# Scores of a head pair in three full PSUM tiles, and three score regions per two pairs

## The chip, the cores and the metric

The kernel runs on one core of one Trainium2 chip. The metric is the device time of one execution in microseconds (us); a kernel's time is the median of several runs.

## What is computed

Blockwise causal attention over 8 batches of 8 heads (576 positions, head size 64, mask blocks of 64), then a layer of two products whose larger value goes through a third. Inputs and output are fp32.

```python
scores = q @ k.T / sqrt(64)                  # per batch and head
scores = where(pos_i // 64 >= pos_j // 64, scores, -1e9)
attn = exp(scores - max); attn = attn / (sum(attn) + 1e-9)
a = attn @ v                                 # [8, 8, 576, 64]
x = a.transpose(0, 2, 1, 3).reshape(4608, 512)
out = maximum(x @ w1, x @ w2) @ w_out        # w1, w2: 512x1024; w_out: 1024x512
```

## The kernel before

All matmuls are in bf16. The order of the work on every engine is written out by hand: each engine's queue runs in the order in which the source calls come.

**Attention.** Two heads that share 128 partitions (64 each) are a pair `p`; there are 32 pairs, four in a batch, and two neighbouring pairs are a group `g` (16 groups). For each pair:

- q and k come in on SP's queue as fp32 (`load_qk`, L109; for later groups a one-column memset on POOL holds the load back, L116), and POOL casts them to bf16 (`cast`, L127). TensorE transposes them (`transposes`, L302: 18 matmuls for q or for k of a whole group), DVE and ACT copy the result to `qT` and `kT` (L309). The table `T_AT` (L459) gives each pair `s` of the main loop one such step: q of the next group for even `s`, k of the next group for odd `s`.
- `scores` (L315) computes keys by queries: the stationary operand is a chunk of 128 keys (64 rows of head dimension by 128 columns), and the moving operand is the run of queries that may see it. The two heads of the pair are two matmuls on the two halves of the partitions. 576 keys are five chunks, the last of 64 keys; its missing 64 columns are zeros, for which `kT` is 64 columns longer (L95). The query runs are 576, 448, 320, 192 and 64 columns long, 1600 in all.
- ACT takes the exponential of a PSUM tile of scores into `aT` (`exp`, L325), and POOL sets to zero the half of a diagonal block that the mask forbids (`mask`, L330).
- A pair's 1600 columns go through PSUM in four tiles from the pool `ps_s`, which holds two tiles of two banks each. `burst_a` (L360) fills two of them with 512 columns per head, `burst_b` (L371) a third with 512 and a fourth with the 64 of the last chunk; each then has its exps and masks.
- `av` (L382) multiplies `aT` with v, which has a column of ones that gives the sum (24 + 6 matmuls of 65 columns, 128x128 weights, L398), and DVE divides (L404, L405). `x_out` (L410) transposes two pairs' results into `xT` (L420, L422). This runs `LAG = 2` pairs behind the scores.

**The layer.** `h_unit` (L181) makes 128 columns of `max(x w1, x w2)` for a span of tokens: four matmuls of up to 512 columns for each of the two (L196), DVE takes them out (L203, L205). `y_unit` (L209) makes 128 tokens of the output: eight matmuls of 512 columns (L214), taken out by ACT (DVE for the first two spans, L220) and stored on SP's queue. `fill(n)` (L280) issues the next `n` steps of this list, in units of one 512-column matmul, as far as tokens are ready. The pool `ps_m` (four tiles of one bank) serves transposes, `av`, `x_out`, h and y alike.

**The main loop** (L547) runs over pairs `s` from 4 to 31: `x_out` if one is due, `burst_a`, a fill of about half of `n`, the transposes of `T_AT`, `burst_b`, the copies of the transposes, `pool_work(s)` (L442: loads and casts for later groups, v loads), `av` of pair `s - 2` in two parts with a short fill between, and the rest of the fill. `fill_of` (L435) sets `n` so that the ready work is spread until the next batch's tokens are ready. Pairs 0 to 3 stand ahead of the loop in an order of their own (L467 to L544).

Of the kernel before, what the change touches and what calls it, by code (L numbers as in the profile page):

```python
# [8 lines left out]
FP32 = mybir.dt.float32  # L9
BF16 = mybir.dt.bfloat16  # L10
AF = mybir.ActivationFunctionType
# [3 lines left out]
def kernel(  # L15
# [10 lines left out]
    nc = tc.nc  # L26

    B, H, S, D = q.shape
    P = 128
    BLK = 64  # L30
    HP = H // 2
    NPAIR = B * HP
# [5 lines left out]
    scale = 1.0 / float(D) ** 0.5  # L38
# [6 lines left out]
    NG = NPAIR // 2  # L45
    GPB = HP // 2

    CB = [0, 448, 768, 960, 1024]  # L50
    AW = 1600
    APAD = 64
    NCH = 5
# [5 lines left out]
    def a_col(p, c, t):  # L59
        if p >= HP:  # L60
            return CB[c] + t * P
        late = t * P >= QCUT
        return t * P + {
            0: 384 - QCUT if late else 0, 1: 704 - QCUT if late else 256 - P,
            2: 1024 - QCUT, 3: 1408 - 3 * P, 4: 1344 - 4 * P,
        }[c]
# [9 lines left out]
    tiles = [(carry[i] + w) // P for i, (_, w) in enumerate(spans)]  # L76

    wpool = ctx.enter_context(tc.tile_pool(name="wpool", bufs=1))
    ring = ctx.enter_context(tc.tile_pool(name="ring", bufs=1))
# [7 lines left out]
    ps_s = ctx.enter_context(tc.tile_pool(name="ps_s", bufs=2, space=bass.MemoryType.PSUM))  # L87
# [4 lines left out]

    NV, NA, NT = 3, 4, 4
    qT_r = [ring.tile([P, S], BF16, name=f"qT{r}") for r in range(NT)]
    kT_r = [ring.tile([P, S + APAD], BF16, name=f"kT{r}") for r in range(NT)]  # L95
    vv_r = [ring.tile([P, NCH, H, D + 1], BF16, name=f"vv{r}") for r in range(NV)]
    aT_r = [ring.tile([P, 2, AW + APAD], BF16, name=f"aT{r}") for r in range(NA)]
    xT = ring.tile([P, NDM, NTOK + BLK], BF16, name="xT")
# [24 lines left out]
    def cast(nm, g, parts):  # L123
        t = raws.pop((nm, g)).rearrange("p s (t d) -> p t s d", d=D)
        qk_n[nm, g] = n = qkn.tile([P, RPP, 2, D], BF16, name=f"{nm}n")
        for copy, j0, j1 in parts:
            copy(out=n[:, j0:j1], in_=t[:, j0:j1])  # L127

    def load_v(b, c):
        rows = min(P, S - c * P)  # L130
        nc.gpsimd.dma_start(  # L131
            out=vv_r[b % NV][:rows, c, :, :D],
            in_=v[b, :, c * P:c * P + rows, :].rearrange("h p d -> p h d"),
        )

# [23 lines left out]
    make_identity(nc, ident)  # L159
    for r in range(NV):  # L160
        nc.vector.memset(vv_r[r][:, :, :, D:D + 1], 1.0)
        nc.vector.memset(vv_r[r][BLK:, NCH - 1, :, :], 0.0)
    for r in range(NT):
        nc.vector.memset(kT_r[r][:, S:], 0.0)
    for r in range(NA):
        nc.vector.memset(aT_r[r][BLK:, :, CB[4] + 512:], 0.0)
        nc.vector.memset(aT_r[r][:BLK, :, AW:], 0.0)
    cast("q", 0, ((dve, 0, 7), (pool, 7, RPP)))
    cast("k", 0, ((act, 0, 5), (dve, 5, RPP)))
    for c in range(2):  # L170
        load_v(0, c)
# [101 lines left out]
    def ready():  # L273
        n, total = at[0], 0.0
        while n < len(steps) and steps[n][1] <= done_tokens[0]:
            total += steps[n][2]
            n += 1
        return int(total)

    def fill(n):  # L280
        while n > 0 and at[0] < len(steps) and steps[at[0]][1] <= done_tokens[0]:
            u, _, cost = steps[at[0]]
            next(u)
            n -= cost
            at[0] += 1
# [28 lines left out]

    def scores(p, ps, col, c, q0, w, m=P):  # L315
        qT, kT = qT_r[p % NT], kT_r[p % NT]
        for hh in range(2):
            r = slice(hh * D, (hh + 1) * D)
            nc.tensor.matmul(  # L319
                ps[:m, hh, col:col + w], kT[r, c * P:c * P + m], qT[r, q0:q0 + w],  # L320
                start=True, stop=True,
            )

    def exp(p, ps, w, a0, m=P):
        nc.scalar.activation(  # L325
            out=aT_r[p % NA][:m, :, a0:a0 + w], in_=ps[:m, :, :w], func=AF.Exp, scale=scale,
        )

    def mask(p, a0, eng=None):
        (eng or nc.gpsimd).memset(aT_r[p % NA][BLK:, :, a0:a0 + BLK], 0.0)  # L330

    def burst(p, parts, a0):
        u = ps_s.tile([P, 2, 512], FP32, name="ps_s", tag="s")
        w = 0
        for c, q0, n in parts:
            scores(p, u, w, c, q0, n)
            w += n
        exp(p, u, w, a0)
# [18 lines left out]
        for a in (1024, 1408):  # L357
            mask(p, a, eng)

    def burst_a(p):  # L360
        u0 = ps_s.tile([P, 2, 512], FP32, name="ps_s", tag="s")
        scores(p, u0, 0, 0, 0, 512)
        u1 = ps_s.tile([P, 2, 512], FP32, name="ps_s", tag="s")
        scores(p, u1, 0, 0, 512, 64)
        scores(p, u1, 64, 1, 128, 448)
        exp(p, u0, 512, 0)
        mask(p, 0)
        exp(p, u1, 512, 512)
        mask(p, 576)

    def burst_b(p):  # L371
        u2 = ps_s.tile([P, 2, 512], FP32, name="ps_s", tag="s")
        scores(p, u2, 0, 2, 256, 320)
        scores(p, u2, 320, 3, 384, 192)
        u3 = ps_s.tile([P, 2, 512], FP32, name="ps_s", tag="s")
        scores(p, u3, 0, 4, 512, 64)
        exp(p, u2, 512, 1024)
        mask(p, 1024)
        mask(p, 1344)
        exp(p, u3, 64, 1536, m=BLK)  # L380

    def av(p, ts):  # L382
        b, hp = divmod(p, HP)
        vv = vv_r[b % NV]
        a = aT_r[p % NA]
        n = len(ts)
        h0 = hp // 2 * 4 + hp % 2
        if p % 2 == 0 and ts[0] == 0:
            xps[p // 2] = xpool.tile([P, NCH, 2, 2, D], BF16, name="xp")
        xp = xps[p // 2]  # L390
        po = ps_m.tile([P, n, 2, D + 1], FP32, name="ps_o", tag="m")
        n_mm = 2 * sum(t + 1 for t in ts)
        mm = 0
        for gi, t in enumerate(ts):
            for hh in range(2):
                for c in range(t + 1):
                    a0 = a_col(p, c, t)
                    nc.tensor.matmul(  # L398
                        po[:, gi, hh, :], a[:, hh, a0:a0 + P], vv[:, c, h0 + 2 * hh, :],
                        start=(mm == 0), stop=(mm == n_mm - 1),  # L400
                    )
                    mm += 1
        rec = small.tile([P, 3, 2, 1], FP32, name="rec")
        nc.vector.reciprocal(rec[:, :n, :, 0], po[:, :, :, D])  # L404
        nc.vector.tensor_mul(  # L405
            xp[:, ts[0]:ts[0] + n, :, p % 2], po[:, :, :, :D],
            rec[:, :n].to_broadcast([P, n, 2, D]),
        )
# [23 lines left out]
    LAG = 2  # L432
    KEEP = 6

    def fill_of(s):  # L435
        if s >= NPAIR - LAG:
            return 27
        left = 10 - s if s < 10 else 4 - (s - 2) % 4
        return -(-max(0, ready() - KEEP) // left)


    def pool_work(s):  # L442
        g, i = divmod(s, 2)
        if s == 4:
            pass
        elif s == 5:
            load_qk(5, (SP, SP), gated=True)
            cast("q", 4, ((pool, 0, RPP),))
        else:
            if i == 1 and g + 3 < NG:  # L450
                load_qk(g + 3, (SP, SP), gated=True)
            if g + 1 + i < NG:
                cast("kq"[i], g + 1 + i, ((pool, 0, RPP),))
            nb, j = divmod(s + 2, HP)
            if nb < B:
                for c in ((0, 1), (2, 3), (4,), ())[j]:
                    load_v(nb, c)
# [4 lines left out]
    def t_pair(s):  # L462
        outs = [transposes(nm, g, (dve, act)) for nm, g in T_AT.get(s, [])]
        return lambda: [f() for f in outs]
# [15 lines left out]
    for c in range(2, NCH):  # L480
        load_v(0, c)
# [62 lines left out]
    fill(3)  # L544

    x_due = []
    for s in range(HP, NPAIR):  # L547
        g, i = divmod(s, 2)
        if x_due:
            x_out(x_due.pop())  # L550
        n = fill_of(s)
        burst_a(s)
        if s == HP:
            av(3, [2, 3, 4])
            fill(5)
            x_out(1, 2, NCH)
            n = fill_of(s)
        n_a = n // 2 if n > 12 else n * 3 // 5
        n_b = n // 6
        fill(n_a)  # L560
        copy_out = t_pair(s)
        burst_b(s)
        copy_out()
        pool_work(s)
        if s >= HP + LAG:
            p = s - LAG
            av(p, [0, 1])
            fill(n_b)
            av(p, [2, 3, 4])
            if p % 2:  # L570
                x_due.append(p // 2)
        else:
            fill(n_b)
        fill(n - n_a - n_b)
    for p in range(NPAIR - LAG, NPAIR):
        if x_due:
            x_out(x_due.pop())
        av(p, [0, 1])
        fill(5)
        av(p, [2, 3, 4])  # L580
        fill(11)
    x_out(NG - 1)
    fill(len(steps))
# [36 lines left out]
```

The softmax here doesn't subtract the row's maximum and nothing guards it: scores larger than these inputs give would overflow.

## Time and profile before

| what | value |
|---|---|
| runs | 288.96, 289.13, 289.14 us; median 289.13 us |
| the profiled execution | 288.79 us, of which the span from the first to the last instruction is 286.7 us |
| granted TensorE clock | 1.000 |
| TensorE busy | 280.0 us, 98% of the span, 3197 matmuls |
| DVE, ACT, POOL busy | 186.7, 137.0, 101.5 us |
| L196 (h), L214 (y) | 140.7 and 69.6 us on TensorE |
| L398 (attention by v), L319 (scores) | 40.5 and 34.7 us on TensorE |
| L325 (exp) on ACT | 128 instructions, 100.3 us |

Times in the profile are us from the start of the span unless marked ns. PE is TensorE's matmul row, PEld its weight loads. A group's line gives the source line, the engine, the operation, what it writes and reads, the size of the stationary operand in rows*columns, the moving operand, and the count. Matmuls are pipelined: the end of one in the records lies after the start of the next, so the distance of two starts is what a matmul takes from the engine. In a timeline the columns are start, length and the group of like instructions that follow each other; brackets hold the idle time of that engine ahead of it and what ended it.

### The profile page before, as it was taken

What the parts mean: (1) busy time and instruction counts of PE and PEld (TensorE: products, weight loads), DVE (VectorE), ACT (ScalarE), POOL (GpSimd) and SP (SyncE); (2) the same over time, 40 slices, a digit from 0 to 9 for tenths busy, and PEclk for the clock granted to TensorE, in tenths of its full rate; (3) what the DMA queues carried; (4) which work ended last, traced back from release to release, by engine and by line L of the source; (5) the groups of instructions that cost most, each with busy time, mean ns of one, the idle gap of its engine ahead of it and who ended that gap; (6) DMA issues with size and microseconds to landing.
All of it is one profiled execution on the core that took longest, in us unless ns stands there. A gap on an engine that the chain in (4) does not pass through costs nothing.

```text
span 286.7 us, 7670 instructions
## 1 busy us (share of the span) xinstructions
PE 280.0 (98%) x3197; PEld 146.1 (51%) x3197; DVE 186.7 (65%) x390; ACT 137.0 (48%) x194; POOL 101.5 (35%) x243
## 2 busy tenths in 40 slices
PE   7799999999999999999999999999999999999995
PEld 3457666555554545545445445454554554444443
DVE  6867878578785666766665666566665766455430
ACT  3786575775665455555545555545545100010112
POOL 2995547547535432344225532543111000000000
PEclk9999999999999999999999999999999999999999
DMA  7999999977954692479266684555101011011114
GB/s 266 259 210 233 169 259 257 247 231 86 192 133 82 141 144 88 156 77 237 49 201 75 171 115 105 130 59 67 43 37 39 37 39 74 37 63 49 53 60 146
DMA packets 55939, 36.67 MB, mean 128 GB/s; under 512 B 38752, under 2 KB 43232, under 8 KB 55904
## 3 DMA queue, kind: packets, MB, share of 16 engines
q0 software_dynamic: 41728, 7.87, 34.0%
q1 hardware_dynamic: 13760, 27.66, 28.4%
q10 hardware_dynamic: 416, 0.66, 0.7%
q8 instruction: 25, 0.41, 0.6%
q14 instruction: 10, 0.08, 0.1%
HBM read 34.60 MB, written 9.44 MB: 154 GB/s over the span
## 4 chain that ended last, share of the span: by engine, by line
PE 93%; DMA 4%; DVE 1%; POOL 0%; issue 0%; ACT 0%
PE ps_h L196 44%; PE ps_y L214 21%; PE ps_o L398 12%; PE ps_s L319 8%; DMA vv<-in_v_dram 2%; PE ps_qT L302 2%; DMA qraw<-in_q_dram 2%; PE ps_xe L420 2%; PE ps_kT L302 2%; PE ps_w L291 1%; PE ps_y L230 1%; PE ps_xo L422 0%; DVE g L205 0%; DVE xp L405 0%; POOL vv L131 0%; DVE qT L309 0%
## 5 line engine op out<-in xcount | busy, mean ns | idle before, releaser
L196 PE MATMUL ps_h<-xT,w_sb 128*128 128x512 bf16 (+3 forms) x640 | 140.7, 358 | 0.1
L325 ACT ACTIVATE aT<-ps_s 128x1024 bf16<-128x1024 f32 (+3 forms) x128 | 100.3, 832 | 59.5 <-PE ps_s L319 56.9
L196 PEld LDWEIGHTS <-w_sb 128*128 128x128 bf16 x640 | 57.7, 98 | 55.6 <-issue 5.5
L203 DVE CAST h<-ps_h 128x512 bf16<-128x512 f32 (+3 forms) x80 | 50.9, 636 | 44.6 <-PE ps_h L196 42.9
L214 PE MATMUL ps_y<-wo_sb,g 128*128 128x512 bf16 x280 | 69.6, 379 | 0.0
L330 POOL MEMSET aT<- 64x128 bf16 x124 | 22.7, 200 | 107.7 <-ACT aT L325 107.3
L220 ACT COPY y<-ps_y 128x512 f32<-128x512 f32 x31 | 18.2, 586 | 81.3 <-PE ps_y L214 58.8
L205 DVE TENSOR_TENSOR g<-h,ps_h 128x512 bf16<-128x512 bf16 (+3 forms) x80 | 50.5, 631 | 9.1 <-PE ps_h L196 7.4
L398 PEld LDWEIGHTS <-aT 128*128 128x128 bf16 x960 | 33.8, 98 | 14.8 <-DVE xp L405 7.6
L398 PE MATMUL ps_o<-vv,aT 128*128 128x65 bf16 x960 | 40.5, 194 | 0.3
L214 PEld LDWEIGHTS <-g 128*128 128x128 bf16 x280 | 25.5, 98 | 27.6 <-issue 3.2
L319 PE MATMUL ps_s<-qT,kT 64*128 64x64 bf16 (+6 forms) x400 | 34.7, 271 | 0.9 <-ACT kT L309 0.7
L131 POOL DMA_DIRECT2D vv<-in_v_dram x40 | 33.7, 847 | 0.0
L405 DVE TENSOR_TENSOR xp<-ps_o,rec 128x256 bf16<-128x256 f32 (+1 forms) x64 | 31.4, 491 | 2.2
L319 PEld LDWEIGHTS <-kT 64*128 64x128 bf16 x400 | 15.9, 94 | 15.2 <-issue 9.3
L404 DVE RECIPROCAL rec<-ps_o 128x4 f32<-128x4 f32 (+1 forms) x64 | 11.8, 184 | 15.1 <-PE ps_o L398 14.8
L127 POOL CAST qn<-qraw 128x1152 bf16<-128x1152 f32 (+1 forms) x15 | 16.5, 1102 | 7.2 <-DMA qraw<-in_q_dram 4.5
L127 POOL CAST kn<-kraw 128x1152 bf16<-128x1152 f32 x15 | 17.2, 1146 | 3.7 <-DMA kraw<-in_k_dram 2.9
L186 POOL COPY g<-g 128x512 bf16<-128x512 bf16 x8 | 4.9, 614 | 37.9 <-DVE g L205 37.8
L425 DVE COPY xT<-ps_xe 128x640 bf16<-128x640 bf16 (+2 forms) x18 | 8.1, 452 | 11.6 <-PE ps_xe L420 11.1
L309 DVE COPY qT<-ps_qT 128x576 bf16<-128x576 bf16 x17 | 12.9, 757 | 2.0 <-PE ps_qT L302 0.7
L309 DVE COPY kT<-ps_kT 128x576 bf16<-128x576 bf16 x17 | 12.8, 754 | 1.8 <-PE ps_kT L302 0.8
(41 smaller groups left out, 113.9 us busy)
## 6 DMA issues: line engine op xcount, KB each, us to landing
qraw<-in_q_dram SPq DMA_DIRECT2D x16, 576.0 KB, 4.2
out_dram<-y SPq DMA_DIRECT2D x35, 256.0 KB, 2.1
kraw<-in_k_dram SPq DMA_DIRECT2D x15, 576.0 KB, 6.1
vv<-in_v_dram POOLq DMA_DIRECT2D x32, 128.0 KB, 6.7
w_sb<-in_moe_w_dram POOLq DMA_DIRECT2D x4, 256.0 KB, 6.5
w_sb<-in_moe_w_dram POOLq DMA_DIRECT2D x2, 512.0 KB, 10.8
wo_sb<-in_moe_w_out_dram POOLq DMA_DIRECT2D x2, 512.0 KB, 12.0
kraw<-in_k_dram ACTq DMA_DIRECT2D x1, 576.0 KB, 5.4
```

Source lines behind the costliest of these rows:

```text
L127: copy(out=n[:, j0:j1], in_=t[:, j0:j1])
L131: nc.gpsimd.dma_start(out=vv_r[b % NV][:rows, c, :, :D], in_=v[b, :, c * P:c * P + rows, :].rearrange("h p d -> p h d"),)
L196: nc.tensor.matmul(pt[:, :w], w_sb[:, c, f * P:(f + 1) * P], xT[:, c, t0:t0 + w], start=(c == 0), stop=(c == NDM - 1),)
L203: nc.vector.tensor_copy(out=h1[:, :w], in_=pt[:, :w])
L205: nc.vector.tensor_max(g[:, f, m:m + w], h1[:, :w], pt[:, :w])
L214: nc.tensor.matmul(py[:], g[:, f, s * P:(s + 1) * P], wo_sb[:, f, :], start=(f == 0), stop=(f == NFF - 1),)
L309: copies[i](out=t[:, :S].rearrange("q (p j) -> q p j", j=RPP), in_=pts[i].rearrange("q j p -> q p j"),)
L319: nc.tensor.matmul(ps[:m, hh, col:col + w], kT[r, c * P:c * P + m], qT[r, q0:q0 + w], start=True, stop=True,)
L325: nc.scalar.activation(out=aT_r[p % NA][:m, :, a0:a0 + w], in_=ps[:m, :, :w], func=AF.Exp, scale=scale,)
L330: (eng or nc.gpsimd).memset(aT_r[p % NA][BLK:, :, a0:a0 + BLK], 0.0)
L398: nc.tensor.matmul(po[:, gi, hh, :], a[:, hh, a0:a0 + P], vv[:, c, h0 + 2 * hh, :], start=(mm == 0), stop=(mm == n_mm - 1),)
L405: nc.vector.tensor_mul(xp[:, ts[0]:ts[0] + n, :, p % 2], po[:, :, :, :D], rec[:, :n].to_broadcast([P, n, 2, D]),)
```

## The change

- A pair's scores go through three PSUM tiles of 512 columns (`tile_0`, `tile_1`, `tile_2`). `tile_0` and `tile_1` are the two tiles of `burst_a`.
- The last key chunk is now keys 448 to 575: 128 keys, the upper 64 of which are the ones that are left. Its rows of v go to partitions 64 to 127, and the lower 64 rows of that chunk of v are zeros. Its 64 columns lie in `tile_2` where chunk 3's first 64 columns lie; of these, chunk 3 needs only the lower 64 partitions (the upper are masked). So chunk 4 is issued first over 128 partitions, then the first 64 columns of chunk 3 as a matmul of 64 stationary columns (`m=BLK`) over the lower 64 partitions, then chunk 2, then chunk 3's other 128 columns. A second, small exp takes the upper 64 partitions of these 64 columns to where `av` reads chunk 4.
- The main loop runs over groups. A group of pairs `a` and `b` has three regions of two tiles each: (0 of a, 1 of a), (2 of a, 0 of b), (1 of b, 2 of b). Matmuls of both tiles come first, then exps and masks. `av` of the pairs of the group before now stands ahead of the transposes and of the second and third region. `fill_of` gives a group's steps; after each of the first two regions come 2/9 of them, between the two parts of `av` 1/18, and the rest after the third region.
- `kT` has no zero columns any more, and fewer parts of `aT` are set to zero at the start.

```diff
-    kT_r = [ring.tile([P, S + APAD], BF16, name=f"kT{r}") for r in range(NT)]
+    kT_r = [ring.tile([P, S], BF16, name=f"kT{r}") for r in range(NT)]
...
-            out=vv_r[b % NV][:rows, c, :, :D],
+            out=vv_r[b % NV][P - rows:, c, :, :D],
...
-        nc.vector.memset(vv_r[r][BLK:, NCH - 1, :, :], 0.0)
-    for r in range(NT):
-        nc.vector.memset(kT_r[r][:, S:], 0.0)
+        nc.vector.memset(vv_r[r][:BLK, NCH - 1, :, :], 0.0)
     for r in range(NA):
-        nc.vector.memset(aT_r[r][BLK:, :, CB[4] + 512:], 0.0)
-        nc.vector.memset(aT_r[r][:BLK, :, AW:], 0.0)
+        nc.vector.memset(aT_r[r][:, :, AW:], 0.0)
...
     def scores(p, ps, col, c, q0, w, m=P):
         qT, kT = qT_r[p % NT], kT_r[p % NT]
+        k0 = min(c * P, S - P)
...
-                ps[:m, hh, col:col + w], kT[r, c * P:c * P + m], qT[r, q0:q0 + w],
+                ps[:m, hh, col:col + w], kT[r, k0:k0 + m], qT[r, q0:q0 + w],
...
+    def tile_0(p):
+        u = ps_s.tile([P, 2, 512], FP32, name="ps_s", tag="s")
+        scores(p, u, 0, 0, 0, 512)
+        return lambda: (exp(p, u, 512, 0), mask(p, 0))
+
+    def tile_1(p):
+        u = ps_s.tile([P, 2, 512], FP32, name="ps_s", tag="s")
+        scores(p, u, 0, 0, 512, 64)
+        scores(p, u, 64, 1, 128, 448)
+        return lambda: (exp(p, u, 512, 512), mask(p, 576))
+
+    def tile_2(p):
+        u = ps_s.tile([P, 2, 512], FP32, name="ps_s", tag="s")
+        scores(p, u, 320, 4, 512, BLK)
+        scores(p, u, 320, 3, 384, BLK, m=BLK)
+        scores(p, u, 0, 2, 256, 320)
+        scores(p, u, 384, 3, 448, P)
+
+        def out():
+            exp(p, u, 512, 1024)
+            nc.scalar.activation(
+                out=aT_r[p % NA][BLK:, :, 1536:AW], in_=u[BLK:, :, 320:320 + BLK],
+                func=AF.Exp, scale=scale,
+            )
+            mask(p, 1024)
+            mask(p, 1344)
+        return out
+
+    def region(*tiles):
+        for out in tiles:
+            out()
...
-    def fill_of(s):
-        if s >= NPAIR - LAG:
-            return 27
-        left = 10 - s if s < 10 else 4 - (s - 2) % 4
+    def fill_of(g):
+        if g == NG - 1:
+            return 54
+        left = 5 - g if g < 5 else 2 - (g - 5) % 2
         return -(-max(0, ready() - KEEP) // left)
...
+    def av_with(p, n):
+        av(p, [0, 1])
+        fill(n)
+        av(p, [2, 3, 4])
+
+    for g in range(GPB, NG):
+        a, b = 2 * g, 2 * g + 1
+        if x_due:
+            x_out(x_due.pop())
+        n = fill_of(g)
+        region(tile_0(a), tile_1(a))
...
+        lo, hi = n // 18, n * 2 // 9
+        for p, tiles in ((a, lambda: (tile_2(a), tile_0(b))), (b, lambda: (tile_1(b), tile_2(b)))):
+            fill(hi)
+            if g > GPB:
+                av_with(p - LAG, lo)
+            else:
+                fill(lo)
+            copy_out = t_pair(p)
+            region(*tiles())
+            copy_out()
+            pool_work(p)
+        if g > GPB:
+            x_due.append(g - 1)
+        fill(n - 2 * (lo + hi))
```

More of the change, by code (lines that the diff above doesn't have):

```diff
@@ L319, in scores, with exp @@
             nc.tensor.matmul(
-                ps[:m, hh, col:col + w], kT[r, c * P:c * P + m], qT[r, q0:q0 + w],
+                ps[:m, hh, col:col + w], kT[r, k0:k0 + m], qT[r, q0:q0 + w],
                 start=True, stop=True,
             )
-    def exp(p, ps, w, a0, m=P):
+    def exp(p, ps, w, a0):
         nc.scalar.activation(
-            out=aT_r[p % NA][:m, :, a0:a0 + w], in_=ps[:m, :, :w], func=AF.Exp, scale=scale,
+            out=aT_r[p % NA][:, :, a0:a0 + w], in_=ps[:, :, :w], func=AF.Exp, scale=scale,
         )
@@ L358, in masks_q @@
             mask(p, a, eng)
[L360 to L380, printed above, removed]
+    def tile_0(p):
[25 more added lines that the diff above has]
+            out()
     def av(p, ts):
@@ L546 @@
     x_due = []
-    for s in range(HP, NPAIR):
-        g, i = divmod(s, 2)
+    def av_with(p, n):
[4 more added lines that the diff above has]
+        a, b = 2 * g, 2 * g + 1
         if x_due:
             x_out(x_due.pop())
-        n = fill_of(s)
-        burst_a(s)
-        if s == HP:
+        n = fill_of(g)
+        region(tile_0(a), tile_1(a))
+        if g == GPB:
             av(3, [2, 3, 4])
@@ L556 @@
             x_out(1, 2, NCH)
[L557 to L574, printed above, removed]
+            n = fill_of(g)
+        lo, hi = n // 18, n * 2 // 9
[12 more added lines that the diff above has]
+        fill(n - 2 * (lo + hi))
     for p in range(NPAIR - LAG, NPAIR):
@@ L577 @@
             x_out(x_due.pop())
-        av(p, [0, 1])
-        fill(5)
-        av(p, [2, 3, 4])
+        av_with(p, 5)
         fill(11)
```

## The prediction

> **What bounds the kernel now.** I read the page's busy times and its chain of work first: they say which engine sets the end.
>
> ```profile
> PE 280.0 (98%) x3197; PEld 146.1 (51%) x3197; DVE 186.7 (65%) x390; ACT 137.0 (48%) x194; POOL 101.5 (35%) x243
> PE 93%; DMA 4%; DVE 1%; POOL 0%; issue 0%; ACT 0%
> ```
>
> The chain is TensorE's for 93%, and no other engine is busy over 65%. A busy TensorE may still be slower than its streams, so next comes its timeline in the steady stretch (start, length, then the group):
>
> ```profile
> 153.26 0.61 PE L319 MATMUL ps_s<-qT,kT 64*128 64x512 bf16 x6
> 153.80 2.76 PE L196 MATMUL ps_h<-xT,w_sb 128*128 128x512 bf16 x12
> 156.50 0.44 PE L302 MATMUL ps_kT<-ident,kn 64*128 64x64 bf16 x18
> 156.77 0.41 PE L319 MATMUL ps_s<-qT,kT 64*128 64x320 bf16 x6
> 157.12 0.36 PE L398 MATMUL ps_o<-vv,aT 128*128 128x65 bf16 x6
> 157.31 0.59 PE L196 MATMUL ps_h<-xT,w_sb 128*128 128x512 bf16 x2
> 157.78 0.59 PE L214 MATMUL ps_y<-wo_sb,g 128*128 128x512 bf16 x2
> 158.33 0.91 PE L398 MATMUL ps_o<-vv,aT 128*128 128x65 bf16 x24
> 159.08 1.46 PE L214 MATMUL ps_y<-wo_sb,g 128*128 128x512 bf16 x6
> 160.37 0.59 PE L196 MATMUL ps_h<-xT,w_sb 128*128 128x512 bf16 x2
> ```
>
> Take differences of starts. L214 x6 takes 1.29, so a 512-column matmul takes 0.216 (and one of w columns w/512 of it; a pair of 64-row matmuls runs side by side as one; 64 columns take 0.029). Then L196 x12 should take 2.59, but the 64-row transposes follow after 2.70. The score burst at 156.77 should take 0.136 + 0.082 + 0.029 = 0.247, but L398 follows after 0.35. So each change between 128-row and 64-row weights costs 0.096 (the starts of single matmuls), in either direction, and transposes to scores (18 in 0.27), both 64*128, cost nothing. Two real waits remain per pair: L214 at 157.78 comes 0.04 late, and L398 at 158.33 0.12 late. The view of waits names the second:
>
> ```profile
> PEld L398 <- DVE xp L405: 7.6, 17, 0.5
> ```
>
> The second attention-value group takes the PSUM slot of the first and waits for its eviction. Last, ACT and POOL around one burst, because the change packs their work:
>
> ```profile
> 161.69 1.94 ACT L325 ACTIVATE aT<-ps_s 128x1024 bf16<-128x1024 f32 x2 [0.48 <-PE ps_s L319]
> 165.21 1.18 ACT L325 ACTIVATE aT<-ps_s 128x1024 bf16<-128x1024 f32 x2 [1.58 <-PE ps_s L319]
> 166.28 0.63 ACT L309 COPY qT<-ps_qT 128x576 bf16<-128x576 bf16 x1
> ```
>
> ```profile
> 166.28 0.35 POOL L330 MEMSET aT<- 64x128 bf16 x2 [2.41 <-ACT aT L325]
> 166.70 1.14 POOL L127 CAST kn<-kraw 128x1152 bf16<-128x1152 f32 x1
> ```
>
> A full exp takes 1.02 and the next starts 0.92 after it; after the small one ACT goes on 0.15 later. The k cast starts 0.26 after the last mask's start and takes 1.14. Now its transposes come most of a pair later, so nobody waits for it.
>
> **What the Trainium skill says.** "TensorEngine Tiling (Array Packing)", Key Properties: changing the tiling mode, not just the tile, drains TensorE; its list has 64×128 and 64×64 as different modes. The trace agrees for 128x128 against 64x128 (0.096); it has no 64x64 weights. "TensorE: Matmul & The Clock Gate", Weight-path perf modes: fast weight load needs 128 weights; its section on LDWEIGHTS gives columns/1.2 ns, so 53 ns for 64. No run here shows that. "PSUM — Partial Sum Buffer", Engine vs sequencer instructions: ScalarE, VectorE and GpSimdE queues are strict FIFO. The trace agrees: masks, cast and v loads start in the order written.
>
> **The change part by part.** Groups g are of two pairs, a and b. The order of the changed instructions is read from the two built programs. Exps, masks and all matmuls except one pair per head pair are as many as before; before the group loop and after its end both orders are equal, so all the difference lies in g = 2 to 15.
>
> 1. *Fewer bursts.* Before, a group has four stretches in 64-row mode (after x_out, after the transposes twice, and burst_a of b alone); after, three. Counted over the program: 150 changes of row mode before, 122 after. 28 × 0.096 = −2.69.
>
> 2. *Chunk 3 in two pieces, one with 64 weights.* tile_2 issues chunk 4 (64x128 weights), then 64 columns of chunk 3 with m=64 (the built program gives these 56 matmuls the tile size 64x64), then chunks 2 and 3 with 64x128. Columns stay the same; streams are 0.029 + 0.056 for 0.082, 28 × 0.002 = +0.06. But the mode changes twice per pair: 56 changes. Their price isn't in the trace. From below 0, if the weights are loaded ahead as between the transposes and the scores; a gain is excluded, as nothing is removed here. From above 0.12, if half of the 53 ns comes on top. I take the nearest row, 0.096, as the skill calls this a mode change like the one measured: 56 × 0.096 = +5.38 (0 to +6.7).
>
> 3. *Slot waits on DVE.* Attention-value groups now stand before the transposes, and the second takes another slot. The old wait (0.04 + 0.12 twice in a group, g = 7 to 14) goes: 8 × 0.32 = −2.5. In g = 2 to 6 some 0.9 of single waits stand in the trace; I take off 0.5. What is late next: the second transpose tile now waits for the first group's eviction. From the last matmul of that group TensorE has 0.43 + 0.75 + 0.10 and DVE takes some 0.2 + 0.2 + 0.42, so it is covered unless a 0.69 cast stands between; up to 0.1 per group, in the range.
>
> 4. *The k cast comes late.* pool_work(a), with the cast of k for group g+1, stands behind region (2a,0b), so behind b's first mask, so behind three exps on ACT. Its transposes are in t_pair(b), now just one fill and one av later. Let 0 be the start of tile_0(b)'s matmuls. tile_2's last matmuls start at −0.06, its exp at about 0.3 (0.37 after them, as from 156.91 to the exp at 157.28). The second full exp starts 1.07 later and ends at 2.4; mask at 2.5 (0.12), cast at 2.75, end 3.9, TensorE can go on at 3.95. TensorE itself arrives after 0.31 (tile_0 and the mode change), hi steps, six matmuls (0.19), lo steps, 24 matmuls (0.75) and a mode change (0.10): g = 3 with 8+2 steps of 320 columns at 0.136: 2.71, wait 1.24; g = 4 with 5+1 at 0.216: 2.65, wait 1.30; g = 5 and 6 with 7+1: 3.08, wait 0.87 each; g = 7 to 14 with 10+2: 3.94, wait 0 to 0.1, I take 0.05. Sum 4.3 + 0.4 = +4.7. g = 2 has its casts from before the loop. In the short groups the second av also waits for ACT's qT copy (end at 2.9); that lies inside the same wait.
>
> 5. *At nothing:* y copies on ACT queue behind 2.6 of exps and a copy; in g = 7 to 14 the copy ends near 3.7, the transposes that take its slot come at 3.94, cover 0.2. v loads are issued behind the cast in the same order and used two pairs later; the q and k loads on SP likewise. Eight memsets fewer on DVE at the start end before the first q data does (it lands at 5.77), which sets the start. The v rows of chunk 4 go to the other 64 partitions in equal number.
>
> Sum: −2.69 + 0.06 + 5.38 − 2.5 − 0.5 + 4.7 = +4.45. The profiled execution took 288.79 (span 286.7 and 2.1 around it); it would take 293.2. The median of the runs, 289.13, is 0.34 above, and gives 289.13 + 4.4 = **293.5**.
>
> **Rivals.** *The column change is free (faster).* The 64x64 weights sit in the same row groups, and TensorE loads them ahead. Then item 2 is 0.06 and the time is 288.1. For it: nothing in this trace shows a price. Against it: 128x128 to 64x128 also only drops part of the array, and pays 0.096 each way. It decides at 0.93 / 56 = 0.017 per change: below, the kernel gets faster. *The cast is in time (no change).* If POOL or ACT run earlier than this chain, item 4 is 0: 288.8. For it: spans on POOL are rough. Against it: the wait hangs on three exps in a row, whose times are firm, and in four groups it is 0.9 or more. *More slots collide (slower still).* T copies, y copies and evictions share four slots, and ACT's queue is 2.6 long after two of three regions; 0.15 per region over 42 regions is some 2: 295.5 to 296.
>
> **How the numbers follow.** Forecast 0.70, free column change 0.12, cast in time 0.08, more collisions 0.10. About 0.2% is what a measurement of this kernel can tell from no change. Faster by more: the first rival and a little of the second, 0.13; within: 0.08; slower: 0.79. The range leaves out the free column change (0.12) and the top of the collisions (0.06): 288.8 to 295.8.
>
> **What would show it.** Single starts around the 64x64 matmuls about 0.1 later than their streams; a wait of the kT transposes for POOL's kn, long in g = 3 to 6 and near none after; no wait of L398 on DVE's xp; three score stretches per group. By this working a steady group (15.55 now, from 84.03 to 99.58 in the chain) changes by 4 × 0.096 − 2 × 0.096 − 0.32 + 0.05 = −0.08: item 2 just eats items 1 and 3, and the loss lies in g = 3 to 6. A steady group shorter by 0.4 or more would say that the column change is free. If instead g = 3 to 6 keep their length, item 4 is wrong.

## The result, and the profile after

| | before | after |
|---|---|---|
| median of the runs | 289.13 us (4 runs, 288.96 to 289.16) | 297.34 us (4 runs, 297.11 to 297.54) |
| ratio | | 1.0285, 95% interval 1.0267 to 1.0303 |
| profiled execution, its span | 288.79, 286.7 us | 297.43, 295.4 us |
| granted TensorE clock | 1.000 | 1.000 |

The changed kernel is slower by 2.85%, 8.2 us, where 4.4 was forecast. The time lies above the forecast range, too. The page's busy times and chain of the changed kernel:

```profile
PE 278.8 (94%) x3207; PEld 154.4 (52%) x3253; DVE 187.6 (64%) x382; ACT 140.7 (48%) x194; POOL 101.3 (34%) x243
PE 84%; DMA 5%; issue 4%; POOL 3%; ACT 2%; DVE 2%; ACTq 0%; POOLq 0%
```

TensorE's busy time is nearly what it was, 1.2 less, but the span grew by 8.7: TensorE's row has more gaps, and POOL is in the chain with 3% where it had none. Part of this is only in the records. The program has 3253 matmuls (the count of weight loads), the page has 3207, and the ones that lack are mostly the first after a burst of scores. Such a gap shows as "0.16 <-issue", and part of the chain's 4% of "issue" is of this kind. So I read distances of starts again, not gaps. The timeline of TensorE in the steady stretch:

```profile
94.35 0.50 PE L300 MATMUL ps_qT<-ident,qn 64*128 64x64 bf16 x18
94.66 0.88 PE L318 MATMUL ps_s<-qT,kT 64*128 64x64 bf16 x10
95.69 0.38 PE L194 MATMUL ps_h<-xT,w_sb 128*128 128x512 bf16 x1 [0.16 <-issue]
95.91 1.89 PE L212 MATMUL ps_y<-wo_sb,g 128*128 128x512 bf16 x8
97.64 0.35 PE L409 MATMUL ps_o<-vv,aT 128*128 128x65 bf16 x6
97.82 0.59 PE L194 MATMUL ps_h<-xT,w_sb 128*128 128x512 bf16 x2
98.39 0.90 PE L409 MATMUL ps_o<-vv,aT 128*128 128x65 bf16 x24
99.33 0.43 PE L300 MATMUL ps_kT<-ident,kn 64*128 64x64 bf16 x18
99.60 0.86 PE L318 MATMUL ps_s<-qT,kT 64*128 64x64 bf16 x12
100.62 0.38 PE L194 MATMUL ps_h<-xT,w_sb 128*128 128x512 bf16 x1 [0.16 <-issue]
```

The second attention-value group at 98.39 now follows the two h matmuls after 0.57, where those need 2 × 0.216 = 0.43. So a wait of 0.14 stands there, until ACT's copy of qT, below, ends at 98.34 and gives its PSUM slot back. (The view of waits names no cause for it; the copy follows from these two times and from the order in which the program takes its four slots.) The k transposes at 99.33 follow 24 matmuls of attention by value after 0.94, where before 24 such matmuls took 0.75 until the next work; with 0.10 for the row change about 0.1 is left. That one is in the view of waits, by the name that was forecast:

```profile
PEld L300 <- POOL kn L128: 5.9, 12, 1.6
```

Twelve waits, one in each of g = 3 to 14, the longest 1.6. (TensorE's weight row also counts time in which earlier matmuls still ran; the stall of the matmuls themselves, from single starts, sums to 5.2.) The stretches in 64-row mode are three per group, and the wait of the attention-value matmuls for DVE's `xp`, 7.6 in 17 times before, is out of the view. What ACT and POOL do in this stretch:

```profile
95.44 1.02 ACT L324 ACTIVATE aT<-ps_s 128x1024 bf16<-128x1024 f32 x1 [2.81 <-PE ps_s L318]
96.49 0.27 ACT L381 ACTIVATE aT<-ps_s 64x128 bf16<-64x128 f32 x1
96.79 1.02 ACT L324 ACTIVATE aT<-ps_s 128x1024 bf16<-128x1024 f32 x1
97.71 0.63 ACT L307 COPY qT<-ps_qT 128x576 bf16<-128x576 bf16 x1
```

```profile
97.87 0.20 POOL L329 MEMSET aT<- 64x128 bf16 x1 [0.94 <-ACT aT L324]
98.13 1.14 POOL L128 CAST kn<-kraw 128x1152 bf16<-128x1152 f32 x1
```

This is the chain of step 4, link by link: exp of `tile_2`, small exp, exp of `tile_0(b)`, mask, cast, ended at 99.27, and the transposes at 99.33. In the short groups it is plain to see. TensorE in g = 4, where the transposes wait for `kn` until 59.61:

```profile
57.24 0.90 PE L409 MATMUL ps_o<-vv,aT 128*128 128x65 bf16 x24
59.61 0.44 PE L300 MATMUL ps_kT<-ident,kn 64*128 64x64 bf16 x18 [1.47 <-POOL kn L128]
```

Where the time came from, by the distance of one group's `x_out` to the next in the two traces. The middle column is what steps 1 to 4 of the prediction give for that group (per group −0.19 for step 1 and +0.38 for step 2, the 0.5 of step 3 spread evenly over g = 2 to 6):

| groups | before → after | forecast | measured |
|---|---|---|---|
| start until `x_out` of g = 2 | 29.47 → 30.32 | 0 | +0.85 |
| g = 2 and 3 | 19.82 → 21.23 | +1.4 | +1.41 |
| g = 4 | 10.11 → 12.03 | +1.4 | +1.92 |
| g = 5 | 11.90 → 13.17 | +1.0 | +1.27 |
| g = 6 | 11.83 → 13.17 | +1.0 | +1.34 |
| g = 7 to 14, each | 15.55 → 15.76 | −0.08 | +0.21 |
| g = 15 | 15.99 → 16.22 | +0.2 | +0.23 |
| end | equal | 0 | 0 |

The pattern is the forecast one, and g = 5 to 14 each lost 0.3 more than forecast. That g = 2 and 3 meet the forecast is luck. The new order hands out the fill differently: counted in units of 512 columns, the h and y matmuls of g = 2 and 3 are 53, before 55, and those of g = 4 are 25, before 23 (read from experiment 5, which has the same fill and lacks no record). That moves 2 × 0.216 = 0.43 from the one row to the other: for equal work g = 2 and 3 lost 1.84, and g = 4 lost 1.49. The start isn't a fixed cost of the change: in the traces of the ten experiments below, whose work up to the loop is nearly the changed kernel's, it takes 29.5 to 32.2, while w and v are still coming in.

### The profile page after: what moved, and what is told of

The parts are those of the page before. It is cut to its first block, busy times and chain, and to the rows that moved or that the text cites. A ratio compares the mean times of both kernels' runs of the same rounds, so it can differ in the third digit from the quotient of the medians.

```text
span 295.4 us, 7720 instructions
## 1 busy us (share of the span) xinstructions
PE 278.8 (94%) x3207; PEld 154.4 (52%) x3253; DVE 187.6 (64%) x382; ACT 140.7 (48%) x194; POOL 101.3 (34%) x243
## 4 chain that ended last, share of the span: by engine, by line
PE 84%; DMA 5%; issue 4%; POOL 3%; ACT 2%; DVE 2%; ACTq 0%; POOLq 0%
PE ps_h L194 39%; PE ps_y L212 20%; PE ps_s L318 9%; PE ps_o L409 8%; DMA w_sb<-in_moe_w_dram 5%; PE ps_w L289 3%; PE ps_qT L300 2%; ACT aT L324 2%; PE ps_kT L300 2%; PE ps_xe L431 2%; POOL kn L128 2%; POOL aT L329 1%; PE ps_y L228 1%; DVE qT L307 1%; DVE qn L128 0%
## 5 line engine op out<-in xcount | busy, mean ns | idle before, releaser
L194 PE MATMUL ps_h<-xT,w_sb 128*128 128x512 bf16 (+3 forms) x604 | 133.8, 357 | 4.0 <-issue 3.2
L324 ACT ACTIVATE aT<-ps_s 128x1024 bf16<-128x1024 f32 (+2 forms) x100 | 95.9, 993 | 70.7 <-PE ps_s L318 69.2
L212 PE MATMUL ps_y<-wo_sb,g 128*128 128x512 bf16 x273 | 65.5, 379 | 0.8 <-issue 0.5
L409 PEld LDWEIGHTS <-aT 128*128 128x128 bf16 x960 | 37.0, 98 | 15.2 <-issue 4.1
L212 PEld LDWEIGHTS <-g 128*128 128x128 bf16 x280 | 26.9, 98 | 32.2 <-issue 1.1
L318 PE MATMUL ps_s<-qT,kT 64*128 64x64 bf16 (+7 forms) x456 | 39.0, 262 | 1.2 <-ACT kT L307 0.7
L318 PEld LDWEIGHTS <-kT 64*128 64x128 bf16 (+1 forms) x456 | 17.8, 95 | 11.7 <-issue 6.0
```

The lines of the kernel that those rows point to most:

```text
L194: nc.tensor.matmul(pt[:, :w], w_sb[:, c, f * P:(f + 1) * P], xT[:, c, t0:t0 + w], start=(c == 0), stop=(c == NDM - 1),)
L212: nc.tensor.matmul(py[:], g[:, f, s * P:(s + 1) * P], wo_sb[:, f, :], start=(f == 0), stop=(f == NFF - 1),)
L318: nc.tensor.matmul(ps[:m, hh, col:col + w], kT[r, k0:k0 + m], qT[r, q0:q0 + w], start=True, stop=True,)
L324: nc.scalar.activation(out=aT_r[p % NA][:, :, a0:a0 + w], in_=ps[:, :, :w], func=AF.Exp, scale=scale,)
L409: nc.tensor.matmul(po[:, gi, hh, :], a[:, hh, a0:a0 + P], vv[:, c, h0 + 2 * hh, :], start=(mm == 0), stop=(mm == n_mm - 1),)
```

## The experiments

The theory after the trace: three costs, which can be undone one by one. The matmuls with 64x64 weights cost about 0.22 per pair. The cast of k comes late. And ACT's small exp holds up both its neighbours, which makes the same chain longer. The main rivals: the records mislead and all of the loss is waiting, or the lost time belongs to the start or to the new order of the queues as a whole. The kernel before, run beside each set of experiments, took 288.9 to 289.45 (medians); differences are taken by the ratios.

**1. No 64x64 weights.**

```diff
-        scores(p, u, 320, 3, 384, BLK, m=BLK)
+        scores(p, u, 320, 3, 384, BLK)
```

> The changed kernel, but the 64 columns of chunk 3 are computed with 128 stationary columns, so that TensorE never holds 64x64 weights (chunk 4's scores are overwritten: that part of the result is left out). Streams, exps, masks and order are the same. Theory (in the changed trace, entering 64x64 costs 0.093, leaving it 0.121 and the next matmul 0.010, 0.225 per pair): 28 x 0.225 = 6.3 us less, 291.0. Rival (the starts of the records mislead, the whole loss is waiting): 297.3, unchanged. Waits of the kT transposes for the k cast stay as they are in both.

291.04 us (290.84 to 292.46, 9 runs); ratio 1.0065 (1.0044 to 1.0086). Against 1.0285 that is 6.4 less, or 0.227 per pair. The same two regions of TensorE in this kernel:

```profile
92.94 0.65 PE L318 MATMUL ps_s<-qT,kT 64*128 64x64 bf16 x10
93.75 0.38 PE L194 MATMUL ps_h<-xT,w_sb 128*128 128x512 bf16 x1 [0.16 <-issue]
...
97.66 0.63 PE L318 MATMUL ps_s<-qT,kT 64*128 64x64 bf16 x12
98.45 0.38 PE L194 MATMUL ps_h<-xT,w_sb 128*128 128x512 bf16 x1 [0.16 <-issue]
```

From the first score to the h record it is 0.81 and 0.79, against 1.03 and 1.02 after the change: 0.22 to 0.23 per region, with the same columns. In the changed kernel's single starts entering 64x64 costs 0.093, leaving it 0.121, and the next matmul 0.010 more. The waits for the cast are the same as without the edit (0.107 in steady groups, 1.25 and 1.53 in g = 3 and 4), so the two costs are apart.

**2. The cast of k one region earlier.**

```diff
             copy_out = t_pair(p)
+            if p == a and g > GPB and g + 1 < NG:
+                cast("k", g + 1, ((pool, 0, RPP),))
             region(*tiles())
...
-            if g + 1 + i < NG:
-                cast("kq"[i], g + 1 + i, ((pool, 0, RPP),))
+            if i == 1 and g + 2 < NG:
+                cast("q", g + 2, ((pool, 0, RPP),))
```

> The changed kernel, but POOL casts k of the next group ahead of region (2 of a, 0 of b), so ahead of its masks. Theory (TensorE waits at the kT transposes for the cast, 1.25 + 1.53 + 0.79 + 0.78 in g = 3 to 6 and 8 x 0.107 after; in g = 3 and 4 ACT's copy of qT, on a slot that the transposes take, keeps some 0.3 and 0.6): about 4.3 us less, 293.0. Rival (the cast only hides a wait for the PSUM slots behind the same exps): under 1 us less, 296.5 or more.

293.0 us (292.63 to 294.79, 4 runs); ratio 1.0134 (1.0088 to 1.0181): 4.4 less. No wait for `kn` is left in the loop. But the transposes don't start at once in g = 3 and 4, and here is TensorE in g = 4:

```profile
59.00 0.20 PE L300 MATMUL ps_kT<-ident,kn 64*128 64x64 bf16 x1
59.60 0.42 PE L300 MATMUL ps_kT<-ident,kn 64*128 64x64 bf16 x17 [0.40 <-ACT qT L307]
```

They now wait for the PSUM slot that ACT's copy of qT gives back, which stands behind the same three exps. For the same reason the second attention-value group waits 0.33 in g = 5 and 6 and 0.14 in g = 7 to 14. ACT's chain, not POOL alone, sets what is left.

**3. The three new tiles in the old order of the loop.**

```diff
+    for s in range(HP, NPAIR):
...
+        region(tile_0(s), tile_1(s))
...
+        fill(n_a)
+        copy_out = t_pair(s)
+        region(tile_2(s))
+        copy_out()
+        pool_work(s)
```

The rest of the loop and `fill_of` are those of the kernel before.

> The three tiles per pair with the chunk 4 layout, but in the order of the kernel before (tiles 0 and 1, half of the fill, transposes, tile 2, then av). Theory (the column change costs 0.225 per pair wherever it stands; the late k cast belongs to the new order): 289.1 + 6.3 = 295.4, and no wait for the k cast. Rival (the new order is what costs, the new tiles are free): 289.1.

293.6 us (293.07 to 294.44, 4 runs); ratio 1.0146 (1.0106 to 1.0185), less than expected. The cast is in time, as expected, and a steady group takes 15.76. That is 0.21 above the kernel before, while two pairs' column changes are 0.45. The view of waits shows where the rest went:

```profile
PEld L409 <- DVE xp L416: 6.3, 17, 0.5
```

In this order the second attention-value group waits for DVE anyway, 0.12 per pair. The column changes make TensorE later by themselves, and the wait shrinks to 0.036; another 0.03 per pair goes at the first y matmul ahead of it, which came late too. Half of the cost is hidden behind waits that were there.

**4. The small exp over all partitions.** What it then writes to the lower 64 partitions meets zeros in v.

```diff
-                out=aT_r[p % NA][BLK:, :, 1536:AW], in_=u[BLK:, :, 320:320 + BLK],
+                out=aT_r[p % NA][:, :, 1536:AW], in_=u[:, :, 320:320 + BLK],
```

> The changed kernel, but the small exp runs over all 128 partitions (the lower half meets zero rows of v). In the changed trace the small exp starts 1.05 us after the big one and the next 0.30 after it, against 0.92 and 0.15 in the kernel before. Theory (an exp on partitions 64 to 127 doesn't overlap with its neighbours): the k cast comes 0.25 us earlier in 12 groups, 2.6 to 3 us less, 294.5. Rival (the gap comes from two exps that read the same PSUM tile): no change, 297.3.

294.33 us (293.71 to 294.98, 4 runs); ratio 1.0171 (1.0125 to 1.0216): 3.3 less. ACT at the same place as above:

```profile
94.09 1.02 ACT L324 ACTIVATE aT<-ps_s 128x1024 bf16<-128x1024 f32 x1 [2.80 <-PE ps_s L318]
95.01 0.27 ACT L381 ACTIVATE aT<-ps_s 128x128 bf16<-128x128 f32 x1
95.17 1.03 ACT L324 ACTIVATE aT<-ps_s 128x1024 bf16<-128x1024 f32 x1
```

Twice the partitions, and the three exps start 0.92 and 0.16 apart, not 1.05 and 0.30. The waits for the cast fall to 1.00, 1.28, 0.53 and 0.52 in g = 3 to 6 and to about none after; a steady group takes 15.51.

**5. The corner with zeros in the weights.** An extra tile `kz` holds keys 384 to 447, 64 columns of zeros, and keys 512 to 575; two matmuls with 128 weights add up in PSUM, so the result is whole and there are no 64x64 weights. It costs two small copies per pair.

```diff
...
-        scores(p, u, 320, 4, 512, BLK)
-        scores(p, u, 320, 3, 384, BLK, m=BLK)
+        for z0, q0 in ((0, 384), (BLK, 512)):
...
+                    u[:, hh, 320:320 + BLK], kz[r, z0:z0 + P], qT[r, q0:q0 + BLK],
+                    start=(z0 == 0), stop=(z0 == BLK),
...
```

> The changed kernel, but the shared 64 columns of tile 2 are made by two 128-column weights that accumulate: chunk 3's first 64 keys beside 64 zero columns, and 64 zero columns beside chunk 4's keys (two small copies per pair into an extra tile hold them). The result is whole, and no 64x64 weights remain. Theory (0.225 per pair is the price of the column change): 297.3 - 6.3 = 291.0, as with the wide chunk 3. Rival (zero columns and the copies on DVE and ACT cost what they save): 294 or more.

290.87 us (290.55 to 292.36, 4 runs); ratio 1.0081 (1.005 to 1.0111), the same as experiment 1 within the intervals. So it is the 64x64 weights that cost, not which columns are computed; the number of matmuls is the same in the changed kernel and in both experiments.

**6. The 64x64 matmuls last in their tile.** In b's region the next work is then a 128-row matmul, so that leaving 64x64 and changing the rows fall together.

```diff
         scores(p, u, 320, 4, 512, BLK)
-        scores(p, u, 320, 3, 384, BLK, m=BLK)
         scores(p, u, 0, 2, 256, 320)
         scores(p, u, 384, 3, 448, P)
+        scores(p, u, 320, 3, 384, BLK, m=BLK)
```

> The changed kernel, but the 64x64 matmuls come last in tile 2. After tile 2 of pair b the 128-row work follows, so that one of its two column changes falls together with a change of row mode that is paid anyway; for pair a nothing changes. Theory (each change of tile size costs about 0.1, whichever way): 14 x 0.12 to 0.13 = 1.7 us less, 295.6. Rival (the price hangs on the 64-column load itself, not on the number of changes): 297.3.

294.39 us (294.31 to 294.51, 4 runs); ratio 1.0193 (1.0175 to 1.0212), 2.7 less, where 1.7 was expected. The end of b's region:

```profile
98.20 0.75 PE L318 MATMUL ps_s<-qT,kT 64*128 64x64 bf16 x12
98.88 0.82 PE L194 MATMUL ps_h<-xT,w_sb 128*128 128x512 bf16 x3
```

One change of 0.120, from 64x64 straight to 128x128, takes the place of two, 0.11 less in each of 14 groups. The rest wasn't foreseen: in region (2 of a, 0 of b) the exps start some 0.1 earlier against the end of the region's matmuls. So one wait per group is 0.10 shorter: that for the cast in g = 3 to 6, that for the slot of ACT's copy in g = 7 to 14.

**7. Experiments 5, 4 and 2 together.**

> Zero columns in place of the 64x64 weights, the small exp over all partitions, and the k cast ahead of the region. Theory (the three losses are separate and add up): 297.3 - 6.3 - 2.9 - 2.6 = 285.5, faster than the kernel before by 3.6: what remains of the change is fewer row changes (2.7) and no wait on DVE's eviction, less some slot waits. Rival (with these gone TensorE meets the next wait on the four slots): 288 to 289.

284.81 us (284.21 to 285.19, 4 runs); ratio 0.9859 (0.9842 to 0.9876). It computes the whole result and beats both kernels. Its page's busy times, where the line numbers are up to 13 higher:

```profile
PE 275.8 (97%) x3253; PEld 152.0 (54%) x3253; DVE 189.0 (67%) x414; ACT 140.3 (50%) x222; POOL 101.8 (36%) x243
```

POOL's cast and TensorE's transposes of the same k in a steady group:

```profile
87.31 1.15 POOL L129 CAST kn<-kraw 128x1152 bf16<-128x1152 f32 x1
```

```profile
91.72 0.90 PE L422 MATMUL ps_o<-vv,aT 128*128 128x65 bf16 x24
92.54 0.44 PE L303 MATMUL ps_kT<-ident,kn 64*128 64x64 bf16 x18
```

The cast ends 4.08 ahead of its transposes, and these follow the attention-value matmuls after 0.82, row change included. A steady group takes 15.07, which is 0.48 less than in the kernel before. This is steps 1 and 3 of the prediction, alone at last: −2 × 0.096 − 0.32 and +0.035 for the first attention-value group's eviction, −0.48. From g = 4 on, two waits of 0.33 in g = 5 and 6 and one of 0.29 in g = 4 are left, beside short ones.

**8. The same with the 128-weight matmul of experiment 1 for the zeros.** It asks what the copies into `kz` cost.

> As the one before, but with the wide chunk 3 of the first experiment in place of the zero columns (chunk 4's scores are overwritten: that part is left out), so without the extra copies. Theory: 285.3, equal to the version with zero columns. Rival (the extra copies on ACT stand ahead of work that TensorE waits for): lower than that version by over 1 us.

285.1 us (284.86 to 285.6, 4 runs); ratio 0.9873 (0.9857 to 0.9889). The copies cost nothing that can be measured.

**9. The small exp on the other half.** It tells whether 64 partitions, the same PSUM tile or the upper half hold up ACT.

```diff
-                out=aT_r[p % NA][BLK:, :, 1536:AW], in_=u[BLK:, :, 320:320 + BLK],
+                out=aT_r[p % NA][:BLK, :, 1536:AW], in_=u[:BLK, :, 320:320 + BLK],
```

> The changed kernel, but the small exp takes partitions 0 to 63 in place of 64 to 127 (chunk 4's probabilities are left out). Theory (an exp that doesn't start at partition 0 doesn't overlap with its neighbours on ACT): as with all partitions, 294.3, and starts of 0.92 and 0.15 after the one before. Rival (any half-height exp behind a full one of the same tile is kept apart): 297.3, and starts of 1.05 and 0.30.

294.66 us (294.05 to 295.03, 4 runs); ratio 1.0186 (1.0159 to 1.0213), 2.9 less.

```profile
94.67 1.02 ACT L324 ACTIVATE aT<-ps_s 128x1024 bf16<-128x1024 f32 x1 [2.80 <-PE ps_s L318]
95.59 0.26 ACT L381 ACTIVATE aT<-ps_s 64x128 bf16<-64x128 f32 x1
95.75 1.01 ACT L324 ACTIVATE aT<-ps_s 128x1024 bf16<-128x1024 f32 x1
```

The same 64x128, the same tile, the same columns, and 0.92 and 0.16 again. So what counts is that the operands lie on the upper half alone. The edits move the exp's input in PSUM and its output in SBUF together; which of the two it is wasn't tried.

**10. The old order without 64x64 weights.** Experiments 3 and 1 together.

> Three tiles per pair in the order of the kernel before, with the wide chunk 3 (chunk 4's scores are overwritten: that part is left out), so without 64x64 weights and without the new order. Theory (the old order with the new tiles took 293.6, of which the column change is 6.3): 287.3, under the kernel before, because the second av group no longer waits 0.12 for its slot. Rival (the column change costs less in the old order): 289 or more.

289.73 us (289.17 to 291.24, 20 runs); ratio 1.001 (0.9998 to 1.0023). My theory fell here. It had three tiles alone as a gain; they are worth nothing in the old order.

```profile
PEld L409 <- DVE xp L416: 7.7, 17, 0.5
```

The wait is back at 7.7, where the kernel before has 7.6, and a group takes 15.56. So experiments 3 and 10 differ by 0.0136 in the ratio, 3.9 us, for the same 56 changes that cost 6.4 in the new order. In the old order the other 2.5 lay behind waits; in a steady group the two traces show 0.17 of it at DVE's wait and 0.06 at the y matmuls. It also says what the new order is worth: by itself (experiment 1 against 10) it loses 0.0055, 1.6 us, since the late chain takes more than it gives; with the cast early and the exp mended (8 against 10) it gains 0.0137, 4.0 us.

## Why the prediction was right in mechanism and wrong in size

The sign and the two losses were forecast. The step that failed is the chain of step 4: one link of it measured 1.35 where 1.07 was put, and that cost 2.5. Step 2's price was too low as well, and cost 0.9.

**Step 1 held.** The trace has 122 changes of row mode, at 0.096 each, and experiment 7 shows the gain in its group length.

**Step 2 had the right mechanism and too low a price.** "I take the nearest row, 0.096": entering 64x64 is that (0.093), leaving it is not (0.121, and 0.010 on the next matmul). 0.225 per pair in place of 0.192 gives 28 × 0.225 = 6.3 for the 5.38 + 0.06, +0.9; it is inside the stated bound of 6.7. The Trainium skill's statement that a change of tiling mode drains TensorE ("TensorEngine Tiling (Array Packing)", Key Properties) agrees with experiments 1 and 5 in that the change has a price, 6.4 us for the kernel; a drain as such is in no view. It led to the right side here, and the first rival is out.

**Step 3 held.** The old waits on DVE went, the 0.5 of the early groups being some 0.4 too few. "What is late next" was named: the first transposes wait for the eviction, 0.035 a group.

**Step 4 is where the size failed, in one term of its sum: "The second full exp starts 1.07 later".** This added 0.92 and 0.15 from the kernel before. There the small exp was on the lower 64 partitions; now it is on the upper, starts 1.05 after the big one and lets the next start only 0.30 later, 1.35 in all. From the start of `tile_0(b)` at 95.16 the trace has the second full exp ended at 2.65 (forecast 2.4), the cast from 2.97 to 4.11 (2.75 to 3.9) and TensorE going on at 4.17 (3.95). The rest of the step is right to some hundredths: TensorE comes first in every group. So 0.22 to 0.25 was missing in each of 12 groups. In g = 7 to 14 it turns a chain that just fits (3.94 against 3.95) into one that doesn't: 0.107 for the cast and 0.139 for the slot that ACT's copy holds, 0.245 against 0.05. The waits on this chain sum to 7.2 for the forecast 4.7: 1.46 and 1.53 in g = 3 and 4, 1.12 and 1.11 in g = 5 and 6, and 8 × 0.245. Experiments 4 and 9 give back 3.3 and 2.9 for that one operand.

**Step 5** held, but left out g = 2: there the chain of exps isn't hidden either (`tile_2(b)` waits 0.34 for a score tile, and the k transposes ahead of it 0.12).

The budget of the miss, 8.64 against 4.45 in the profiled executions: step 4 +2.5, step 2 +0.9, g = 2 +0.46, first transposes +0.3, step 3 −0.4, the start +0.85. These are 4.6 for 4.2. Where the 0.85 of the start comes from stays open. That the start takes 29.5 to 32.2 in the ten traces with nearly the same work speaks for scatter; the one with 32.2, of experiment 2, took 294.79 us, and the other three runs of that kernel at most 293.30. But one trace of each kernel can't settle it. The medians differ by 8.2, not 8.64, because the changed kernel's profiled execution lay 0.09 above its median, and the kernel before's 0.34 below.

By the groups' lengths the forecast sign "a steady group −0.08" was wrong by 0.29: 0.07 from step 2, 0.195 from step 4, 0.035 from the first transposes. The rival of more collisions came nearer in size, but by another mechanism: what it blamed, four shared slots, costs 0.139 a group, and it is the same ACT chain that holds the slot: with the exp over all partitions a steady group is 0.25 shorter.

## What to carry to other kernels

A duration from the profile belongs to the operand's place as well as its size: when a small instruction moves to other partitions or another weight shape, price it as unknown in how it overlaps its neighbours, not only in its own length. Where a step just fits (3.94 against 3.95), the cost isn't the middle of a small range but zero or the full error of the chain, times the number of rounds. And a rewrite that looks like a loss may hold a gain: undo its costs one by one, for a cost can hide behind a wait that another part of the rewrite removes.

## What the runs showed of the hardware

- On ACT, an exp of 64x128 on partitions 64 to 127 didn't overlap its neighbours: it started 1.04 to 1.07 after a 1.02 exp in all 28 pairs, and the next instruction started 0.30 after it; experiment 10 shows the same. On partitions 0 to 63 or 0 to 127 (experiments 9 and 4) the two were 0.90 to 0.92 and 0.16. What in the engine does this isn't settled by these runs.
- A change of TensorE from 64x128 to 64x64 weights cost 0.093, back 0.121 and 0.010 on the next matmul; from 64x64 to 128x128 in one step (experiment 6) 0.120. A change of rows alone cost 0.096 either way.
- Two matmuls of 128 weight columns, half of them zeros, that add up in PSUM cost less than one of 128 and one of 64 columns that write the same place: 290.87 against 297.34 us for the kernel, ratios 1.0081 and 1.0285.
